# FNet mixing and channel mix on one core: a tile of its own for one mirrored row, and a new order for the opening's products

## The chip, the cores and the metric

The kernel runs on one core of one Trainium2 chip. The metric is the device time of one execution in microseconds (us), as the median of several executions. The engines of the core have these names in the profile: PE is TensorE (matmuls), PEld its weight loads, DVE is VectorE, ACT is ScalarE, POOL is GpSimd, SP is SyncE.

## What is computed

For an input x of 8 batches, 3072 rows and 256 columns the reference takes the real part of a two-dimensional discrete Fourier transform, and puts the result through a channel mix:

```python
X = np.fft.fft(x, axis=1)
X = np.fft.fft(X, axis=2)
x = X.real
x_prev = x shifted by one row, zeros ahead of the first
xk = mu_k * x + (1.0 - mu_k) * x_prev
xr = mu_r * x + (1.0 - mu_r) * x_prev
k = np.maximum(xk @ w_k, 0.0)          # 256 -> 1024
v = k * k @ w_v                        # 1024 -> 256
r = 1.0 / (1.0 + np.exp(-(xr @ w_r)))  # 256 -> 256
out = r * v
```

## The kernel before

**Folding.** The real part of a transform of real data pairs row s with row S - s and column d with column D - d. The kernel therefore loads every batch twice: `load_p` brings the rows as they are (tile `xp`), and `load_m` gathers the mirrored rows (tile `xm`) with an indirect DMA. `fold` adds the two on DVE into the tile `p` (L147 the bulk, L149 the first column again). A batch has two halves, h = 0 with nine rows for each of 96 partitions and h = 1 with eight. The mirrored tile of a half has eight rows of 256 and a ninth behind them, at element `XM0 + 2048`. For h = 0 the ninth comes by a gather of its own, `load_m0`; for h = 1 only a zero written at the start stands there. There are three `xm` tiles in turn, and "slot 0" is the first of them, which the first half of the first batch uses.

The columns of a row are read backwards from the row behind's first element: the bulk add of `fold(0, 0, 1, 4)` reads elements `XM0 + 2048` down to `XM0 + 1025`. Its first element is thus the first of the ninth row. What it adds there is overwritten by the second, small add.

**The transform in stages.** With Cooley-Tukey steps the transform becomes three kinds of products: `a_sum` or `a_item` (L480, L463/460) multiply `p` by the table `w_pm`; `d_half` or `d_item` (L497) multiply the result `a` by the table `w_eo`; `c_item` (L535) multiplies `g_all` by the table `m_cs`. Each stage's result is copied out of PSUM by ACT (L443) or DVE (L441). `halves`, `diff` and `mix_part` on DVE then make the mixed rows for the channel mix.

**Tables.** All tables are made on the chip. Angles are sums of outer products, `outer` (L287), with one row of weights; DVE scales and wraps them (`m_angles`, `m_wrap`, both L249), and ACT takes the sines (`m_sine`, L400). The table `m_cs` comes in three parts of 5, 4 and 5 columns: `(0, NJ1)`, `(NJ1, NJ2)`, `(NJ2, NJ)`. The vectors mu are loaded as rows, reordered by ACT (`mu_rows`, L196), turned into columns by eight tiny fp32 matmuls (`mu_turn`, L203) and copied to `mu_f` by DVE (L205); `mix_part` reads `mu_f`.

**The channel mix.** The steady part has 192 steps over chunks of 512 output rows: `k_piece` (products L615, ACT's relu L625), DVE's `square` (L632), `v_tile` (L653), `r_item` (L639), `v_out` (L663). The next batches' transform is put between by a table of steps (`at`).

**Order.** The order of instructions on each engine is the program's own order: `pin_order` chains them at the end. So an instruction that waits holds back all that stands behind it on its engine. PSUM tiles come in turn from three slots of 1024 columns (`ps_w`, tile `psW`) and two of 512 (`ps_v`, tile `psV`). All input loads are issued by POOL, in one queue. `keep_busy(n)` issues n matmuls of 512 columns on zeros (L180), whose results nobody reads.

The opening of the program, up to the first product of the channel mix, is written out by hand:

```python
    m_sine(0, NJ1)
    m_first()
    mu_rows(1)
    eo_sine()
    eo_rest()
    keep_busy(8)
    fold(0, 0, 1, 4)
    a_sum(0, 0, 0)
    m_outer(NJ1, NJ2)
    fold(0, 0, 5, 4)
    a_sum(0, 0, 4)
    mu_turn()
    loads()
```

Of the kernel before, what the change touches and what calls it, by code (L numbers as in the profile page):

```python
# [10 lines left out]
FP16 = mybir.dt.float16  # L11
# [9 lines left out]
def _v(ap, extra_offset, free_dims):  # L21
    new_ap = [list(ap.ap[0])] + [[s, c] for (s, c) in free_dims]
    return dataclasses.replace(ap, offset=ap.offset + extra_offset, ap=new_ap)
# [16 lines left out]
def kernel(  # L40
# [18 lines left out]
    NJ, NJ1, NJ2 = 14, 5, 9  # L59

    const = ctx.enter_context(tc.tile_pool(name="const", bufs=1))
# [12 lines left out]
    def ps_slot(kind, n, cols):  # L74
        k = ps_n[kind] % n
        ps_n[kind] += 1
        return psum.tile([P, cols], FP32, name=f"ps{kind}{k}", tag=f"ps{kind}{k}", bufs=1)

    def ps_w():
        return ps_slot("W", 3, 1024)  # L80

    def ps_v():
        return ps_slot("V", 2, 512)
# [23 lines left out]
    V = nc.vector  # L107
    XM0 = 257
    xm_sb = [const.tile([96, XM0 + 2306], FP16, name=f"xm{n}") for n in range(3)]
    idx_4 = const.tile([96, 2], UINT32)  # L110
    idx_8 = const.tile([96, B, 2], UINT32)
    idx_0 = const.tile([96, B], UINT32)
# [10 lines left out]
    def gather(dst, src, idx):  # L123
        nc.gpsimd.indirect_dma_start(dst, None, src, bass.IndirectOffsetOnAxis(ap=idx, axis=0))  # L124

    def load_m(b, h, o, n, idx):
        gather(xm_t[b, h][:, XM0 + o:XM0 + o + 256 * n],
               x.rearrange("b (s r) d -> (b s) (r d)", r=n), idx)

    def load_m0(b):  # L130
        load_m(b, 0, 2048, 1, idx_0[:, b:b + 1])

    def load_xh(b, h):
        x_tiles(b, h)
# [5 lines left out]
    def fold(b, h, q0=0, n=0):  # L140

        n = n or 9 - h
        if (b, h) not in p_t:
            p_t[b, h] = p_pool.tile([96, 9, 256], FP16, name="p")
        p, xp, xm = p_t[b, h], xp_t[b, h], xm_t[b, h]
        o = XM0 + 256 * (8 - h - q0)
        V.tensor_tensor(out=p[:, q0:q0 + n], in0=xp[:, q0:q0 + n],  # L147
                        in1=_v(xm, o + 256, [(-256, n), (-1, 256)]), op=ALU.add)
        V.tensor_tensor(out=p[:, q0:q0 + n, 0], in0=xp[:, q0:q0 + n, 0],  # L149
                        in1=_v(xm, o, [(-256, n)]), op=ALU.add)  # L150
# [15 lines left out]
    mu_f = const.tile([P, 2, 2], FP32)  # L166
# [9 lines left out]
    def keep_busy(n, ps=None):  # L176

        ps = ps or ps_v()
        for _ in range(n):
            nc.tensor.matmul(out=ps[:, 0:512], lhsT=zeros, rhs=_v(zeros, 0, [(0, 4), (1, P)]),  # L180
                             start=True, stop=True)

    keep_busy(5)


    mu_row = const.tile([1, 2, 256], FP32)
# [6 lines left out]
    def mu_rows(a):  # L193
        for p0, f0, step, n in (((0, 0, 1, 1), (1, 2, 2, 63), (64, 1, 2, 64)),
                                ((0, 128, 1, 1), (1, 254, -2, 63), (64, 255, -2, 64)))[a]:
            nc.scalar.activation(out=mu_p[:, a, :, p0:p0 + n],  # L196
                                 in_=_v(mu_row, f0, [(256, 2), (step, n)]), func=AF.Copy)

    def mu_turn():
        ps = ps_w()  # L200
        for a in range(2):
            for i in range(2):
                nc.tensor.matmul(out=ps[:, 2 * a + i:2 * a + i + 1], lhsT=mu_p[:, a, i], rhs=unit,  # L203
                                 start=True, stop=True)
        V.tensor_copy(out=mu_f.rearrange("p a i -> p (a i)"), in_=ps[:, 0:4])  # L205

    for h in range(2):
        x_tiles(0, h)
    for xm in xm_sb:
        V.memset(_v(xm, XM0 + 2048, [(256, 2)]), 0.0)  # L210
    iota = nc.gpsimd.iota
    ueo = const.tile([P, 2, 2, 64], INT32)
    w_eo = const.tile([P, 2, 128], FP16)
# [27 lines left out]
    warm = const.tile([P, 1], FP32)  # L241
    nc.scalar.activation(out=warm, in_=zeros[:, 0:1], func=AF.Sin, bias=0.0, scale=1.0)
    mu_rows(0)
    nc.scalar.activation(out=m_cs.rearrange("p c s t -> p (c s t)").bitcast(FP32),
                         in_=_v(zeros.bitcast(FP32), 0, [(0, 2 * NJ), (1, 64)]), func=AF.Copy)

# [15 lines left out]
    def rv(n, o, *dims):  # L262
        return _v(rw, P * n + o, list(dims))
# [21 lines left out]
    def outer(out, rhs):  # L285
        for n, (row, r) in enumerate(rhs):
            nc.tensor.matmul(out=out, lhsT=rw[:, row], rhs=r, start=n == 0, stop=n == len(rhs) - 1)  # L287
# [3 lines left out]
    ps = ps_w()  # L291
# [37 lines left out]
    def m_outer(j0, j1):  # L329
        ps = ang_ps[j0] = ps_w()  # L330
        n = j1 - j0
        for c in range(2):
            outer(ps[:, 512 * c:512 * c + 64 * n],
                  [(Q2, rv(JR, j0, (1, n), (0, 64))), (RR, rv(TR, 0, (0, n), (1, 64))),
                   (PH + c, rv(ONE, 0, (0, n), (1, 64))),
                   (D0 + c, rv(J0, 0, (1, n), (0, 64)))][:4 if j0 == 0 else 3])
# [5 lines left out]
    def m_wrap(j0, j1):  # L342
        ts(ang[:, :, j0:j1], ang[:, :, j0:j1], TURN - 1, ALU.bitwise_and)

    keep_busy(1)
    m_outer(0, NJ1)
    ts(u_w, ps[:, 0:WA + WB], TURN / 96.0, MUL)
    ts(u_w, u_w, TURN - 1, ALU.bitwise_and)
# [49 lines left out]
    def m_sine(j0, j1):  # L398
        for part, odd in ((hi64, 0), (lo64, 1)):
            nc.scalar.activation(  # L400
                out=m_cs.rearrange("p c (j o) t -> p c j o t", o=2)[part, :, j0:j1, odd],
                in_=ang[part, :, j0:j1], func=AF.Sin, bias=m_pi[part], scale=TWO_PI / TURN)

    def m_first():
        nc.scalar.activation(out=_v(m_cs[hi64], 0, [(2 * NJ * 64, 2)]), in_=zeros[hi64, 0:2],
                             func=AF.Copy)
# [17 lines left out]
    def eo_sine():  # L424
        nc.scalar.activation(out=w_eo.rearrange("p a b -> p (a b)"),
                             in_=ueo.rearrange("p a c b -> p (a c b)"), func=AF.Sin,
                             bias=m_pi, scale=TWO_PI / TURN)
# [11 lines left out]
    def evac(out_ap, in_ap, eng):  # L439
        if eng == "V":  # L440
            V.tensor_copy(out=out_ap, in_=in_ap)  # L441
        else:
            nc.scalar.activation(out=out_ap, in_=in_ap, func=AF.Copy)  # L443

    def a_tile(b):
        a_t[b] = y_pool.tile([P, 2, NU, 64], FP16, name="a")
# [21 lines left out]
    def a_sum(b, h, i0, engs="A"):  # L468


        if (h, i0) == (0, 0):
            a_tile(b)
        ps = ps_w()
        for i in range(4):
            parts = [(h, i0 + i + 1 - h, 0, 2 * WA, 0, 1)]
            if h and i0 + i == 7:
                parts = [(0, 0, 0, WA, WA, 1), (1, 7, 1, WA, 1, 2)]
            for half, q, o, n, w, step in parts:
                for k in range(2):
                    nc.tensor.matmul(out=_v(ps, 256 * i + o, [(2 * WA // n, n)]),  # L480
                                     lhsT=p_t[b, half][:, q, 128 * k:128 * k + 128],
                                     rhs=_v(w_pm[0:96], (WA + WB) * k + w,
                                            [(WA + WB, 2), (step, n // 2)]),
                                     start=(k == 0), stop=(k == 1))
            n = 4 // len(engs)
            if i % n == n - 1:
                evac(_v(a_t[b], 8 * h + i0 + i + 1 - n, [(16, 2 * WA), (1, n)]),
                     _v(ps, 256 * (i + 1 - n), [(1, 2 * WA), (256, n)]), engs[i // n])

    def d_units(b, ps, u0, n, bank):  # L490

        for i in range(n):
            for e in range(2):
                o = bank * e + 128 * i
                nc.tensor.matmul(out=ps[:, o:o + 128],  # L497
                                 lhsT=a_t[b][:, e, 2 * (u0 + i):2 * (u0 + i) + 2, :],
                                 rhs=w_eo[:, e], start=True, stop=True)

    def d_evac(ps, u0, n, bank, eng):
        evac(_v(g_all, 256 * u0, [(64, 2), (128, 2 * n), (1, 64)]),
             _v(ps, 0, [(bank, 2), (64, 2 * n), (1, 64)]), eng)
# [8 lines left out]
    def d_half(b, u, ps, eng):  # L512
        d_units(b, ps, u, 2, 256)
        d_evac(ps, u, 2, 256, eng)
# [159 lines left out]

    m_sine(0, NJ1)
    m_first()
    mu_rows(1)
    eo_sine()
    eo_rest()
    keep_busy(8)  # L680
    fold(0, 0, 1, 4)
    a_sum(0, 0, 0)
    m_outer(NJ1, NJ2)
    fold(0, 0, 5, 4)
    a_sum(0, 0, 4)
    mu_turn()
    loads()
    m_angles(NJ1, NJ2)
    m_wrap(NJ1, NJ2)
    keep_busy(4)  # L690
    fold(0, 1, 0, 4)
    a_sum(0, 1, 0)
    fold(0, 0, 0, 1)
    turn_rows()
    fold(0, 1, 4, 4)
    keep_busy(2)
    a_sum(0, 1, 4, "VA")
    m_outer(NJ2, NJ)
    m_angles(NJ2, NJ)
    d_half(0, 0, ps_v(), "A")  # L700
    d_half(0, 2, ps_v(), "V")
    m_wrap(NJ2, NJ)
    c_item(0, 0, 5, "A", True)
    c_item(0, 5, 4, "A", True)
    m_sine(NJ1, NJ2)
    d_item(0, 1)


# [161 lines left out]
```

## Time and profile before

| what | value |
|---|---|
| three executions | 456.34, 457.2, 458.16 us, median 457.2 us |
| the profiled execution | 457.78 us, of it 456.0 us from its first to its last instruction (the span) |
| mean granted clock of TensorE over the span | 0.973 |
| busy PE, DVE, ACT, POOL | 442.3, 360.6, 327.1, 50.9 us |
| PE busy from 100 to 400 us | 300.0 of 300 us |

A slice of the page's second part is a fortieth of the span, 11.4 us. The chain of waits is followed back from the last instruction; a piece of it that names a PE line is time in which PE was the one worked on. Times inside the profile are counted from the first instruction.

### The profile page before, as it was taken

How to read it: one execution, taken by the hardware profiler on the slowest of the kernel's cores; microseconds unless marked ns; L12 is line 12 of the kernel's file. 1: busy time of each engine (PE TensorE's matmuls, PEld its weight loads, DVE VectorE, ACT ScalarE, POOL GpSimd, SP SyncE). 2: the span in 40 equal slices, each digit the busy share in tenths (PEclk: the TensorE clock that was granted, in tenths of full speed). 3: DMA queues.
4: the chain of work that ended last, by engine and by line, in shares of the span. 5: the costliest groups of instructions: out<-in, count | busy, mean ns of one | idle time of the engine just before them, and what ended most of it. 6: DMA issues, size and time to landing. Idle time of an engine off the chain costs nothing.

```text
span 456.0 us, 8500 instructions
## 1 busy us (share of the span) xinstructions
PE 442.3 (97%) x3479; PEld 314.3 (69%) x3479; DVE 360.6 (79%) x529; ACT 327.1 (72%) x369; POOL 50.9 (11%) x65
## 2 busy tenths in 40 slices
PE   8798999999999999999999999999999999999996
PEld 3455677677777777777777777777777777666764
DVE  5357899998789896998879896998879865997453
ACT  6148788777777777777777777777777777666661
POOL 7560213100400012000400010000000000000000
PEclk9657999999999999999999999999999999999999
DMA  7992567623942258222942253322332322333324
GB/s 127 184 175 49 78 141 122 141 55 72 167 111 58 60 100 173 63 64 55 168 117 52 65 95 93 70 64 53 70 69 48 70 63 53 71 70 69 71 64 99
DMA packets 34507, 40.93 MB, mean 90 GB/s; under 512 B 3906, under 2 KB 30788, under 8 KB 34468
## 3 DMA queue, kind: packets, MB, share of 16 engines
q1 hardware_dynamic: 27524, 25.05, 22.7%
q0 software_dynamic: 6784, 15.21, 21.0%
q8 instruction: 27, 0.44, 0.4%
q10 hardware_dynamic: 160, 0.13, 0.1%
q14 instruction: 12, 0.10, 0.1%
HBM read 30.41 MB, written 25.17 MB: 122 GB/s over the span
## 4 chain that ended last, share of the span: by engine, by line
PE 91%; DVE 3%; ACT 2%; DMA 1%; issue 1%; POOL 1%; POOLq 0%; DVEq 0%
PE psV L653 36%; PE psW L615 35%; PE psW L639 9%; PE psW L535 3%; PE psW L497 3%; PE psW L463 2%; PE psW L480 2%; DMA xm<-in_x_dram,idx 1%; ACT rl L625 1%; PE psW L287 1%; DVE k L632 1%; DVE d L559 0%; DVE x L584 0%; POOL xm L124 0%; ACT pq L443 0%
## 5 line engine op out<-in xcount | busy, mean ns | idle before, releaser
L625 ACT ACTIVATE rl<-psW 128x1024 f16<-128x1024 f32 x192 | 196.4, 1024 | 98.8 <-PE psW L615 93.8
L653 PE MATMUL psV<-wv_sb,k 128*128 128x256 f16 x1536 | 199.5, 273 | 0.0
L615 PE MATMUL psW<-x,wk 128*128 128x512 f16 (+1 forms) x776 | 198.1, 379 | 1.2 <-ACT rl L625 0.7
L653 PEld LDWEIGHTS <-k 128*128 128x128 f16 x1536 | 146.5, 98 | 27.9
L632 DVE TENSOR_TENSOR k<-rl 128x2048 f16<-128x2048 f16 (+1 forms) x98 | 117.6, 1201 | 50.9 <-ACT rl L625 50.6
L615 PEld LDWEIGHTS <-wk 128*128 128x128 f16 x776 | 76.3, 98 | 51.9 <-issue 2.4
L663 DVE SCALAR_TENSOR_TENSOR o<-psV,r 128x512 f32<-128x512 f32 (+1 forms) x97 | 66.1, 682 | 16.2 <-PE psV L653 13.7
L584 DVE TENSOR_TENSOR x<-y,t 128x1536 f16<-128x1536 f16 x60 | 57.5, 959 | 2.1
L639 PE MATMUL psW<-wr,x 128*128 128x256 f16 x384 | 49.8, 273 | 0.0
L644 ACT ACTIVATE r<-psW 128x1024 f16<-128x1024 f32 x48 | 48.9, 1018 | 0.8 <-PE psW L639 0.8
L639 PEld LDWEIGHTS <-x 128*128 128x128 f16 x384 | 37.6, 98 | 14.6 <-issue 0.3
L443 ACT ACTIVATE a<-psW 128x832 f16<-128x832 f32 (+1 forms) x32 | 27.2, 849 | 12.5 <-PE psW L480 12.5
L121 POOL DMA_DIRECT2D xp<-in_x_dram x16 | 9.1, 566 | 209.1 <-DVE p L149 184.4
L124 POOL DMA_INDIRECT xm<-in_x_dram,idx x25 | 31.2, 1247 | 7.6 <-issue 6.4
L443 ACT ACTIVATE pq<-psW 128x768 f16<-128x768 f32 (+5 forms) x32 | 27.5, 859 | 1.8 <-PE psW L535 1.7
L443 ACT ACTIVATE g_all<-psW 128x1024 f16<-128x1024 f32 (+3 forms) x39 | 28.0, 722 | 0.0
L147 DVE TENSOR_TENSOR p<-xp,xm 96x2304 f16<-96x2304 f16 (+3 forms) x19 | 20.9, 1102 | 3.9 <-DMA xm<-in_x_dram,idx 3.8
L551 DVE TENSOR_TENSOR y<-pq 128x960 f16<-128x960 f16 (+5 forms) x38 | 18.6, 532 | 5.0 <-ACT pq L443 4.8
L535 PEld LDWEIGHTS <-g_all 128*128 128x128 f16 (+1 forms) x233 | 15.3, 99 | 9.3 <-ACT g_all L443 1.6
L497 PEld LDWEIGHTS <-a 128*128 128x128 f16 x208 | 15.2, 103 | 7.7 <-issue 1.3
L571 DVE TENSOR_SCALAR t<-d,mu_m 128x1536 f16<-128x1536 f16 x32 | 19.6, 614 | 0.0
L535 PE MATMUL psW<-m_cs,g_all 128*128 128x128 f16 (+2 forms) x221 | 18.1, 222 | 1.2 <-ACT g_all L443 1.2
(100 smaller groups left out, 197.5 us busy)
## 6 DMA issues: line engine op xcount, KB each, us to landing
out_dram<-o SPq DMA_DIRECT2D x190, 128.0 KB, 2.4
xp<-in_x_dram POOLq DMA_DIRECT2D x8, 432.0 KB, 6.4
xp<-in_x_dram POOLq DMA_DIRECT2D x8, 384.0 KB, 4.6
wv_sb<-in_moe_w_v_dram POOLq DMA_DIRECT2D x1, 512.0 KB, 9.0
xm<-in_x_dram,idx POOLq DMA_INDIRECT x25, 7.2
out_dram<-o ACTq DMA_DIRECT2D x2, 64.0 KB, 2.0
out_dram<-o SPq DMA_DIRECT2D x2, 64.0 KB, 2.2
wk<-in_moe_w_k_dram,row_i POOLq DMA_INDIRECT x4, 7.0
```

The lines of the kernel that those rows point to most:

```text
L124: nc.gpsimd.indirect_dma_start(dst, None, src, bass.IndirectOffsetOnAxis(ap=idx, axis=0))
L443: nc.scalar.activation(out=out_ap, in_=in_ap, func=AF.Copy)
L497: nc.tensor.matmul(out=ps[:, o:o + 128], lhsT=a_t[b][:, e, 2 * (u0 + i):2 * (u0 + i) + 2, :], rhs=w_eo[:, e], start=True, stop=True)
L535: nc.tensor.matmul(out=ps[0:m, o:o + 64 * k], lhsT=g_all[:, u, 128 * min(f, 1):128 * min(f, 1) + m], rhs=m_cs[:, f % 2, sl:sl + k], start= ...
L584: V.tensor_tensor(out=dst, in0=_v(y_t[b], 64 * (NSL * a + lo + 3 * m), [(1, n)]), in1=_v(x_t["t", a], 64 * lo, [(1, n)]), op=ALU.subtract ...
L615: nc.tensor.matmul(out=st["k", ds][:, 512 * hs + lo:512 * hs + hi], lhsT=wk_sb[m][a][:, 128 * fc:128 * fc + 128], rhs=xk[:, a, 512 * i + l ...
L625: nc.scalar.activation(out=st["rl"][:, 2 * ds:2 * ds + 2], in_=st["k", ds].rearrange("p (f t) -> p f t", f=2), func=AF.Relu, bias=0.0, sca ...
L632: V.tensor_tensor(out=k2_t[c][:, lo:hi], in0=r, in1=r, op=ALU.mult)
L639: nc.tensor.matmul(out=ps[:, 256 * tb:256 * tb + 256], lhsT=x_t[b, 1, m][:, a, 512 * i + 128 * tb: 512 * i + 128 * tb + 128], rhs=wr_sb[m] ...
L644: nc.scalar.activation(out=st["r", c], in_=ps, func=AF.Sigmoid)
L653: nc.tensor.matmul(out=st["v", tb - h][:, 256 * h:256 * h + 256], lhsT=k2_t[c][:, fc, 128 * tb:128 * tb + 128], rhs=wv_sb[:, fc], start=(f ...
L663: V.scalar_tensor_tensor(out=o.rearrange("p a b -> p (a b)")[:, 0:256 * n], in0=st["v", t0][:, 0:256 * n], scalar=16.0, in1=st["r", c][:, ...
```

## The change

It touches the opening alone, in these parts:

1. The ninth mirrored row of the first half of the first batch is gathered into a tile of its own, `xm_00`, instead of the first `xm` tile. `fold(0, 0, 0, 1)` reads it there. The other folds and the other batches are as before.
2. `keep_busy` at the very start has 8 matmuls instead of 5; the one ahead of `m_outer(0, NJ1)` goes; the block of 8 ahead of the first `a_sum` becomes 7; the blocks of 4 and 2 between the later `a_sum` go.
3. `m_outer(NJ1, NJ2)` goes from between the first two `a_sum` to a place ahead of the block of 7.
4. `mu_rows(1)` goes forward on ACT to stand beside `mu_rows(0)`. `mu_turn` goes behind `m_wrap(NJ1, NJ2)` and `m_sine(NJ1, NJ2)` in the program, and its copy on DVE to `mu_f` is taken out of it and put behind the last `a_sum`.
5. `m_sine(NJ1, NJ2)` goes from behind the first two `c_item` to a place right behind its `m_wrap`.
6. `d_half(0, 0)` and `d_half(0, 2)` now stand ahead of `m_outer(NJ2, NJ)` and `m_angles(NJ2, NJ)`.

```diff
+    xm_00 = const.tile([96, 514], FP16)
...
     def load_m0(b):
-        load_m(b, 0, 2048, 1, idx_0[:, b:b + 1])
+        if b == 0:
+            gather(xm_00[:, 1:257], x.rearrange("b s d -> (b s) d"), idx_0[:, 0:1])
+        else:
+            load_m(b, 0, 2048, 1, idx_0[:, b:b + 1])
...
         o = XM0 + 256 * (8 - h - q0)
+        if (b, h, q0) == (0, 0, 0):
+            xm, o = xm_00, 1
...
-    keep_busy(5)
+    keep_busy(8)
...
-        V.tensor_copy(out=mu_f.rearrange("p a i -> p (a i)"), in_=ps[:, 0:4])
+        return ps
...
+    V.memset(xm_00[:, 257:258], 0.0)
...
     mu_rows(0)
+    mu_rows(1)
...
-    keep_busy(1)
     m_outer(0, NJ1)
...
     m_first()
-    mu_rows(1)
     eo_sine()
     eo_rest()
-    keep_busy(8)
+    m_outer(NJ1, NJ2)
+    keep_busy(7)
     fold(0, 0, 1, 4)
     a_sum(0, 0, 0)
-    m_outer(NJ1, NJ2)
     fold(0, 0, 5, 4)
     a_sum(0, 0, 4)
-    mu_turn()
     loads()
     m_angles(NJ1, NJ2)
     m_wrap(NJ1, NJ2)
-    keep_busy(4)
+    m_sine(NJ1, NJ2)
+    mu_ps = mu_turn()
     fold(0, 1, 0, 4)
     a_sum(0, 1, 0)
     fold(0, 0, 0, 1)
     turn_rows()
     fold(0, 1, 4, 4)
-    keep_busy(2)
     a_sum(0, 1, 4, "VA")
+    V.tensor_copy(out=mu_f.rearrange("p a i -> p (a i)"), in_=mu_ps[:, 0:4])
+    d_half(0, 0, ps_v(), "A")
+    d_half(0, 2, ps_v(), "V")
     m_outer(NJ2, NJ)
     m_angles(NJ2, NJ)
-    d_half(0, 0, ps_v(), "A")
-    d_half(0, 2, ps_v(), "V")
     m_wrap(NJ2, NJ)
     c_item(0, 0, 5, "A", True)
     c_item(0, 5, 4, "A", True)
-    m_sine(NJ1, NJ2)
     d_item(0, 1)
```

## The prediction

> **What bounds the kernel now.** First the page's second part, for where PE lacks work or clock:
>
> ```profile
> PE   8798999999999999999999999999999999999996
> ...
> PEclk9657999999999999999999999999999999999999
> ```
>
> From the fifth slice (46 us) on PE is full at full clock. Time is to be had in the opening alone, and an opening shorter by x ends the kernel earlier by x, if nothing later is short of data. Next, the chain of waits there (start, length, what):
>
> ```profile
> 6.12 6.79 DMA xm<-in_x_dram,idx
> ...
> 13.04 0.70 DVE p L147
> ...
> 14.00 0.89 PE psW L480 x8
> 14.89 1.38 PE psW L287 x6
> 16.26 1.50 PE psW L480 x8
> 17.76 1.81 PE psW L203 x8
> ...
> 19.59 0.16 DVE mu_f L205
> ...
> 20.88 0.70 DVE p L147
> ...
> 23.40 0.85 PE psV L180 x2
> ```
>
> The first fold waits for the gather issued at 6.12, the ninth row's; the eight rows that its sums need were issued at 2.53 and landed 7.1 later, at 9.6. Then PE works in its order, with the angles (L287) and mu (L203) between the sums, and DVE's copy of mu stands ahead of the next fold, whose data had landed by 12.5 (issue 4.48, 8.0 to landing). The waits of the opening say the same:
>
> ```profile
> DVE mu_f L205 <- PE psW L203: 4.9, 1, 4.9
> ...
> DVE p L147 <- DMA xm<-in_x_dram,idx: 3.8, 1, 3.8
> ```
>
> Last the clock. Its record changes at 11.46 (up), 14.87 (down), 35.35, 42.18 and 45.59, all whole multiples of 3.41 us apart. The busy times by these stretches (length, then PE, PEld, DVE, ACT, POOL, clock, DMA share, GB/s):
>
> ```profile
> 4.63:8.05 3.42, 3.21 (x14) 1.74 (x15) 1.94 (x10) 1.20 (x3) 2.78 (x5) 1.00 0.91 160
> 8.05:11.46 3.41, 3.09 (x8) 0.80 (x6) 1.12 (x3) 2.83 (x7) 2.74 (x9) 1.00 1.03 189
> 11.46:14.87 3.41, 0.87 (x9) 0.70 (x10) 1.63 (x4) 0.28 (x3) 2.93 (x4) 1.00 1.08 187
> ...
> 21.70:25.11 3.41, 3.12 (x14) 2.05 (x15) 2.00 (x12) 0.86 (x1) 2.05 (x3) 0.50 1.04 168
> ```
>
> The column of 1.00 ahead of 11.46 is no clock: the 512-column matmuls start every 0.43 there (7.94 to 10.08 is five of them), as at 0.50. 4.63 to 8.05 was busy, but with one-row weights, and brought no full clock; 8.05 to 11.46, with 2.90 of 128-row work (85%), did. 21.70 to 25.11 did not: 2.08 with 96 of 128 rows and 0.85 with 128, by rows 71%. So a stretch counts by rows; it raises the clock somewhere from 71 to 85%. A stretch with 32% (38.77 to 42.18, five k products of 0.216 by their rate there) lost it, one with PE busy for 2.46 (45.59 to 49.00) kept it.
>
> **Parts with one answer.** `mu_rows(1)` (0.6 of ACT) goes to 3.0, where ACT is free from 4.6 to 5.85: nothing. Blocks of zeros whose removal saves only PE time that was waiting (the one of L180 at 3.87): nothing. The longer first block runs from 1.0 to 4.4 (8 x 0.43); the outer products behind it, at 3.24 before, end about 5.1, and DVE reads them at 5.24 at the earliest, since it writes rows until 5.3: nothing, and at most 0.2 if this is short. The new memset: 0.06 of DVE in the free start. POOL issues the same number of loads in the same order; the second batch's second half, which waited for a fold until 22.45, can go at 18.4, but DMA was saturated then (share over 1 in every us from 15 to 36), and one queue serves all: nothing for slot 0, whose last gather lands at 13.8 (7.33 and 6.5).
>
> **The first fold.** It starts at 9.75 (9.6 and the 0.13 that it took at 12.91) instead of 13.04; DVE is free from 9.2. First sums at 10.7 instead of 14.0: 3.3 off the path, if PE is free. Its block of seven stands behind the six angle products (1.28). With the clock's boundaries as in this trace, 1.0 to 4.4 fills 94% of 1.22 to 4.63, so the clock is full to 8.05, the block done at 9.7. At other boundaries all of it runs at half rate: 7.7 + 1.28 + 7 x 0.43 = 12.0, and the first sums lose 1.3 of the 3.3.
>
> DVE now adds while POOL issues loads (9.65 to 12.8). The add of 13.86 ran beside POOL's gather of 13.74 to 14.70 in 0.68, that of 20.88 beside an idle POOL in 0.69: no price. The Trainium skill (SBUF — State Buffer, the section with the port table) says that a DVE instruction with two SBUF inputs and a GpSimd instruction reading SBUF block each other for a whole instruction. The two adds do not show it. By the rule up to 0.95 could come back at each of three folds, 2.9 in all, and the sum would be 452.1.
>
> **From first sum to the first `c_item`,** 14.00 to 29.76 before, at half clock (starts of neighbours subtracted): the angle products between go (1.38); four zeros and the wait behind them, 19.49 to 21.83, go (2.34), since DVE, without mu's copy, folds at 10.57 and 12.65, and that half is ready at 13.55, PE at 15.3 after mu's matmuls (1.8); the two zeros go (0.85), since the last fold is ready at 15.55 and PE comes at 16.7. Against this, the first sums ran in 0.82 at full clock and now take 1.39 (-0.57), and behind the last copy of `a` PE does `d_half` (1.03) and the angles (1.60) in 3.06 instead of 2.93 (-0.13): ACT's copy (0.6), which hid behind the angles, now stands open, and the angles hide the copy of `g_all` instead. 1.38 + 2.34 + 0.85 - 0.57 - 0.13 = 3.9. `c_item` starts at 29.76 - 3.3 - 3.9 = 22.5.
>
> `m_sine(NJ1, NJ2)` (1.45) now runs at 14.6 on ACT, between copies that end at 14.6 and start at 16.9: hidden. From `c_item` on PE was full up to 38.57, so the 1.45 that ACT gains at 32.33 is worth nothing.
>
> **The clock's share.** At this trace's boundaries no stretch from 8.05 to 25.11 holds over 65% (8.05 to 11.46: zeros 1.65, sums 0.57): half clock, 7.2 in all. At boundaries in the middle of the block of seven, zeros and the sums behind them fill over 85% and the clock rises between 12 and 14: after the loss of 1.3 each set of eight sums saves 0.69, mu's about 0.9, the later pieces up to 2, bounded by the folds at 13.55 and 15.55: 8 to 10. Where it rises nowhere: 7.2 - 1.3 = 5.9. One profile doesn't tell where boundaries fall in other runs. I take 8.0, nearest the first two cases, and keep 5.9 and 10.
>
> **Sum.** The profiled execution took 457.8, 0.6 above the median: 449.8 for it, 449.2 against the median.
>
> **Rivals.** *Full clock throughout.* PE is busy from 1.0 to 9.7 and never waits 2 us; were rows no matter, the clock stayed up. Then only data and copies bind: last fold 15.55, sums and copies to 18.1, `c_item` at 19.35, 10.4 earlier, and about 2 more from its products, zeros and k products at full rate until DVE binds: 12.4, or 444.8. Against it: 4.63 to 8.05 and 21.70 to 25.11 above. The Trainium skill (TensorE: Matmul & The Clock Gate, "Why this matters for your kernels") asks only for 4 us of continuous work. The trace disagrees where that work has one row or 96.
>
> *The fold stays tied.* The eight-row gather shares the queue and perhaps the count that the fold waits for; then the first sums stay at 14.0, and only the 3.9 is left: 453.3. For it: what the fold really waits for is inferred. Against: each landing has its own time in the trace.
>
> *Taken back by data.* The next batch's fold came at 44.97, its data at 25.0; the second half's at 53.48, data at 31.7; the next weights land by 34.6. Slack 18 and more: 457 only if something unseen binds.
>
> *Slower.* With the six zeros between the sums gone, the stretches around the first k products could miss the share that raises the clock, and the steady part start at half clock. A step has 0.86 of k and 0.87 of v products at full rate, so each costs 1.73 more; to end 0.5% slower the 8.0 and 2.3 more must go, six steps, 21 us of PE work at half clock: 449.2 + 6 x 1.73 = 459.6. Against it: every stretch with over 85% raised the clock, four zeros and k products still stand together, and steps at half clock are full.
>
> **Numbers.** Forecast 0.78, full clock 0.08, tied 0.07, taken back 0.02, slower 0.05. The range reaches from just above full clock, 445.0, to the tied case, 453.5; it leaves out part of the full clock and the last two, some 0.12. About 0.5%, 2.3 us, is what a measurement of this kernel can tell from no change: faster 0.93, same 0.02, slower 0.05.
>
> **What would show it.** In the changed profile: first L147 near 9.75, released by the gather of 2.53; first L480 at 10.7 to 12.0; no L205 wait of DVE ahead of the second half's fold, which starts by 13; first L535 at 19.5 to 24; L400 near 15; L625 first at 31 to 33 instead of 39. Wrong if the first L480 is still at 14, if the clock stays at 0.50 beyond the first k products, or if DVE or ACT show a new wait of over 1 us between 10 and 22 on mu or the sines.

## The result: about 1.5% faster, a little less than forecast

| | before | after | ratio (95% interval) |
|---|---|---|---|
| first comparison | 457.51 us | 451.47 us | 0.9869 (0.9834 to 0.9905) |
| repeated | 456.97 us | 449.41 us | 0.9835 (0.9805 to 0.9864) |
| repeated again | 457.37 us | 449.47 us | 0.9817 (0.9783 to 0.9850) |

One of the eleven runs of the kernel before in the second comparison took 738.54 us at a mean granted clock of 0.653, and its ratio leaves that run out. The sixteen runs of the changed kernel lie between 446.71 and 452.51, their median is 449.9. The first profiled execution took 450.17, its span 448.4: 7.6 less than before. The forecast of 449.2 lies 2.3 below the first median and within 0.3 of the two later ones.

The page's second part after the change, PE and its clock:

```profile
PE   9889999999999999999999999999999999999995
...
PEclk9778999999999999999999999999999999999999
```

PE is fuller in the first four slices, and from the fifth to the last but one it is as full as before. The first relu of the steady part starts at 31.29 instead of 38.96, 7.7 earlier, and the span is 7.6 shorter: what the opening gains goes through to the end. ACT before and after:

```profile
38.96 2.81 ACT L625 ACTIVATE rl<-psW 128x1024 f16<-128x1024 f32 x3
...
31.29 2.81 ACT L632 ACTIVATE rl<-psW 128x1024 f16<-128x1024 f32 x3
```

The chain of waits in the opening (start, length, what):

```profile
4.50 8.52 DMA xm<-in_x_dram,idx
...
13.53 0.70 DVE p L153
...
16.55 0.70 PE psW L487 x4
...
19.15 0.55 ACT a L450
...
20.78 1.71 PE psW L295 x6
22.49 1.84 PE psW L542 x15
```

The first fold is no longer on it. The chain now begins with the gather for the second half (issued at 4.50) and goes over DVE's folds; mu's products and the copy of mu are gone from it. The line numbers have moved: L487 are the sums (L480 before), L153 the folds, L542 the `c_item` (L535). The first `c_item` starts at 22.42 by the timeline (the chain counts it from 22.49), where before it was this line:

```profile
29.76 1.91 PE L535 MATMUL psW<-m_cs,g_all 128*128 128x64 f16 x15 [0.26 <-ACT g_all L443]
```

The first fold and the first sums in the timeline of DVE and of PE:

```profile
10.27 0.69 DVE L153 TENSOR_TENSOR p<-xp,xm 96x1024 f16<-96x1024 f16 x1 [0.83 <-DMA xm<-in_x_dram,idx]
```

```profile
9.05 3.17 PE L186 MATMUL psV<-zeros 128*128 128x512 f16 x7
12.01 2.40 PE L487 MATMUL psW<-w_pm,p 96*128 96x208 f16 x16
14.34 1.05 PE L209 MATMUL psW<-unit,mu_p 1*128 1x1 f32 x8
```

The fold starts 2.8 earlier than before, but PE comes only when the seven zeros end, at 12.0. The clock record rises at 13.67, falls at 17.09, rises at 27.33, falls once more at 34.15 and is up from 37.57 to 447.16. The two stretches around the rise (length, busy PE, PEld, DVE, ACT, POOL, clock, DMA share, GB/s):

```profile
10.25:13.67 3.42, 3.42 (x15) 2.06 (x14) 2.78 (x7) 1.22 (x6) 3.11 (x4) 1.00 1.11 188
13.67:17.09 3.42, 3.07 (x28) 2.49 (x27) 2.57 (x12) 3.38 (x5) 2.81 (x3) 1.00 0.96 130
```

The first holds zeros and sums (1.79 of zeros and 1.63 of sums with 96 of 128 rows, by rows 88%), the second sums and mu's products at full clock (1.6 of sums, by rows about 35%), and it loses the clock again. The 1.00 of the first stretch is still the missing record; its rate is half.

### The profile page after: what moved, and what is told of

Same layout as the page of the kernel before. It is cut to its first block, busy times and chain, and to the rows that moved or that the text cites. A ratio compares the mean times of both kernels' runs of the same rounds, so it can differ in the third digit from the quotient of the medians.

```text
span 448.4 us, 8492 instructions
## 1 busy us (share of the span) xinstructions
PE 437.5 (98%) x3474; PEld 312.4 (70%) x3474; DVE 361.0 (81%) x530; ACT 327.1 (73%) x369; POOL 51.6 (12%) x65
## 4 chain that ended last, share of the span: by engine, by line
PE 91%; DVE 3%; ACT 2%; DMA 2%; issue 1%; POOL 0%; POOLq 0%; DVEq 0%
PE psV L660 36%; PE psW L622 36%; PE psW L646 9%; PE psW L542 3%; PE psW L504 3%; DMA xm<-in_x_dram,idx 2%; PE psW L470 2%; ACT rl L632 1%; PE psW L487 1%; DVE k L639 1%; DVE d L566 0%; DVE x L591 0%; ACT pq L450 0%; PE psW L295 0%; PE psW L186 0%
## 5 line engine op out<-in xcount | busy, mean ns | idle before, releaser
L153 DVE TENSOR_TENSOR p<-xp,xm 96x2304 f16<-96x2304 f16 (+3 forms) x19 | 20.9, 1102 | 1.3 <-DMA xm<-in_x_dram,idx 1.3
L542 PEld LDWEIGHTS <-g_all 128*128 128x128 f16 (+1 forms) x233 | 15.3, 99 | 9.4 <-ACT g_all L450 1.1
L542 PE MATMUL psW<-m_cs,g_all 128*128 128x128 f16 (+2 forms) x221 | 18.1, 222 | 0.9 <-ACT g_all L450 0.9
```

What stands on the lines that cost most here:

```text
L542: nc.tensor.matmul(out=ps[0:m, o:o + 64 * k], lhsT=g_all[:, u, 128 * min(f, 1):128 * min(f, 1) + m], rhs=m_cs[:, f % 2, sl:sl + k], start= ...
```

## Experiments

**The tile alone.** The kernel before, with `xm_00`:

```diff
+    xm_00 = const.tile([96, 514], FP16)
...
+        if b == 0:
+            gather(xm_00[:, 1:257], x.rearrange("b s d -> (b s) d"), idx_0[:, 0:1])
...
+        if (b, h, q0) == (0, 0, 0):
+            xm, o = xm_00, 1
...
+    V.memset(xm_00[:, 257:258], 0.0)
```

> The kernel before with the own tile for the ninth row alone. Theory (two separate gains, tile and order): the first fold starts at 10.2 instead of 13.04, released by the eight-row gather; the first sums start at 11.1 (the block of eight ends there) instead of 14.0; everything behind, mu's copy ahead of the second half's fold included, comes 2.8 us earlier: 454.7 against 457.5. Rival A (the order does it all, since the wait for mu's copy binds anyway): under 0.5 us of gain. Rival B (the tile does it all): 6 us, 451.5. Rival C (the fold stays tied): first fold at 13, no gain.

Measured: 451.53 against 457.26, ratio 0.9866 (0.9833 to 0.9900), single runs from 450.55 to 452.68. The PE timeline, of the slowest of the four:

```profile
7.57 3.60 PE L186 MATMUL psV<-zeros 128*128 128x512 f16 x8
10.96 1.55 PE L487 MATMUL psW<-w_pm,p 96*128 96x208 f16 x8
12.44 0.82 PE L294 MATMUL psW<-rw 1*128 1x256 f16 x6
13.20 0.89 PE L487 MATMUL psW<-w_pm,p 96*128 96x208 f16 x8
14.01 1.05 PE L209 MATMUL psW<-unit,mu_p 1*128 1x1 f32 x8
```

The times of the theory came (fold 9.59, sums 10.96, 3.0 earlier). Its 454.7 is 3.2 too high, since a second gain came that it did not have. With the wait gone the sums follow the zeros at once, the clock rises at 12.34, and the angles, the second sums and mu's products take 0.76, 0.81 and 0.98 where they took 1.38, 1.49 and 1.80; the first sums, at half, lose 0.66. First `c_item` at 25.12, 4.6 earlier: 3.0 and 1.6. The size is that of rival B, and in the first comparison the whole change (451.47) was no faster than this. The reason is not rival B's: DVE still waits 3.81 for mu's products here, and the order alone gains as well, as the next run shows.

**The order alone.** The changed kernel, the ninth row in the shared tile:

```diff
-    xm_00 = const.tile([96, 514], FP16)
...
-        if (b, h, q0) == (0, 0, 0):
-            xm, o = xm_00, 1
...
```

> The changed kernel without the own tile: the ninth row goes to the shared tile again. Theory: first fold at 13, first sums at 14.0, and only the order's share is left, 3.2 to 3.9 us: 453.6 to 454.3 against 457.5; the second half's fold starts at about 16 instead of 20.9. Rival A (the order does it all): 451.5. Rival B (the tile does it all): 457 to 458.

Measured: 452.79, ratio 0.9897 (0.9868 to 0.9925), first `c_item` at 26.14, 3.6 earlier, span 3.9 shorter. PE:

```profile
14.01 2.96 PE L480 MATMUL psW<-w_pm,p 96*128 96x208 f16 x16 [3.63 <-DVE p L149]
16.89 1.86 PE L203 MATMUL psW<-unit,mu_p 1*128 1x1 f32 x8
```

The second half's fold starts at 15.71 instead of 20.88. The theory's places hold, all at half clock, and the profiled execution (453.83) lies in its range; the median is 0.8 below it. Each part alone gives 4.5 to 5.7 us and both together 6.0 to 7.9, less than the sum. In the profiles the parts bring the first `c_item` 4.6 and 3.6 forward, and both together 7.3, and 6.4 and 8.1 in the two repeats further down. In two of these three the block of seven ends at 12.0, where the block of eight ended at 11.0, which is 1.0 of what is missing. The medians lack more than that; why was not traced.

**Four zeros instead of seven.**

```diff
-    keep_busy(7)
+    keep_busy(4)
```

> The changed kernel with four 512-column zeros instead of seven ahead of the first sums. Theory (the seven hold the first sums up: they end at 12.0 where the fold is ready at 11.2): first sums at 11.2, 0.8 us earlier; the clock then rises in no stretch ahead of 17, so the sums run at half rate and up to 1.9 us come back: between 0.8 faster and 1.1 slower than the changed kernel's 451.5. Rival D (the zeros set nothing, data does): no difference, first sums at 12. Rival E (the zeros are what keeps the opening fast): 2 us or more slower, 453.5 and above.

Measured: 449.61, ratio 0.9832 (0.9806 to 0.9858), its four runs within 0.4. First sums at 10.89 instead of 12.01, but the last sums start at 16.21 instead of 16.55: they wait for the last fold, so only 0.5 of the 1.1 reaches the first `c_item` (21.97). The clock rose all the same (13.16): the expectation that it would not was wrong. Beside all sixteen runs of the changed kernel the time is not told apart.

**The clock by rows.** Zeros with a chosen number of rows ahead of everything (one execution, 502.08 us):

```diff
...
+    for rows, n in ((1, 24), (96, 24), (P, 24), (96, 48), (1, 48)):
+        zeros_rows(rows, n, probe_ps)
     keep_busy(5)
```

> The kernel before with matmuls of 512 columns on zeros put ahead: 24 with one row, 24 with 96 rows, 24 with 128, 48 with 96, 48 with one row (blocks of about 10 us, without a gap). Nothing else differs; it is some 50 us longer. Theory (the clock counts rows): no rise in the first block; the rise comes in the block of 128 rows, or, if the share that raises it lies under 75%, in the first block of 96; it is kept through the second block of 96 and lost within two stretches of 3.41 us in the last block of one row. Rival (busy time counts, whatever the rows): the rise comes within 7 us of the first matmul, and the clock is kept to the end.

By 0.43 and 0.216 a matmul the blocks begin at 1.0, 11.2, 19.6, 24.8 and 35.1. The record rises at 17.66, falls at 38.14. The stretches:

```profile
7.42:10.83 3.41, 3.41 (x10) 1.12 (x8) 0.00 (x0) 0.00 (x0) 2.72 (x9) 1.00 1.05 196
10.83:14.25 3.42, 3.42 (x9) 1.03 (x8) 0.00 (x0) 0.00 (x0) 3.12 (x4) 1.00 1.13 189
14.25:17.66 3.41, 3.41 (x9) 1.21 (x8) 0.00 (x0) 0.00 (x0) 2.49 (x4) 1.00 1.16 149
...
34.72:38.14 3.42, 3.42 (x17) 1.36 (x16) 0.00 (x0) 0.00 (x0) 0.00 (x0) 1.00 0.00 0
38.14:41.55 3.41, 3.41 (x10) 1.17 (x9) 0.00 (x0) 0.00 (x0) 0.00 (x0) 0.50 0.00 0
```

PE is busy throughout. One row brings no rise in 10 us, 96 rows bring it with the first stretch that they fill, and one row loses it with the first stretch that it fills nearly alone. Rows count, and a filled stretch of 96 rows, 75%, is enough. With the 71% of the kernel before, which were not, the share that raises the clock lies between 71 and 75%.

**The copy of mu back ahead of the second half's fold.**

```diff
     mu_ps = mu_turn()
+    V.tensor_copy(out=mu_f.rearrange("p a i -> p (a i)"), in_=mu_ps[:, 0:4])
     fold(0, 1, 0, 4)
...
-    V.tensor_copy(out=mu_f.rearrange("p a i -> p (a i)"), in_=mu_ps[:, 0:4])
```

> The changed kernel with DVE's copy of mu right behind mu's products again, ahead of the second half's fold. Theory (the copy held DVE): that fold starts behind mu's products, at 15.5 instead of 13.5, the last fold at 17.6 instead of 15.7, and the end comes about 2 us later: 453.5. Rival (PE's order holds the sums anyway): the sums of the second half start behind mu's products in both, under 0.5 us.

Measured: 451.13, 1.7 above the changed kernel of the same comparison (449.41). DVE's wait is back, in the list of waits from 8 to 20 us:

```profile
DVE mu_f L697 <- PE psW L209: 2.8, 1, 2.8
```

The fold starts at 15.28 instead of 13.53, the last one at 17.30 instead of 15.70, the first `c_item` at 24.32 instead of 22.42: 1.9. These places are as the theory has them. The span is only 1.0 longer than that of the first profile (449.4 against 448.4), because this execution does not lose the clock a second time behind the first k products (it is up from 30.26 on).

**The zeros back between the sums,** run in two comparisons:

```diff
     mu_ps = mu_turn()
+    keep_busy(4)
...
     fold(0, 1, 4, 4)
+    keep_busy(2)
     a_sum(0, 1, 4, "VA")
```

> The changed kernel with the blocks of four and two zeros back between the later sums. Theory (they now stand on the path): 0.9 to 1.7 us for the four, up to 0.9 for the two, 453 to 454. Rival (they raise the clock and pay for themselves): 451.5 or less, with a record of full clock from 17 on.

> The changed kernel with the blocks of four and two zeros back, again. Theory (zeros cost 2 us where the clock is at half, and where it is up they keep it up and give 4 to 5): single runs fall into two groups, near 446 and from 449 to 452.5; the median beats the changed kernel by 1 us or more. Rival (the two runs at 445.9 were chance): median within 1 us of the changed kernel's.

Measured: 447.46 and 447.43, 2.0 below the median of the changed kernel both times (ratios 0.9791, 0.9752 to 0.9830, and 0.9796, 0.9753 to 0.9839). The intervals overlap those of the changed kernel. The ten runs go from 445.39 to 452.60, and their mean, 448.5, is only 0.65 below the 449.1 of the twelve runs beside them: that the zeros gain is not clear of the spread. In the first profile, of the slowest run of its four (452.45), the clock is at half from 7.72 to 31.61, and there the zeros cost what was expected; PE:

```profile
15.62 1.89 PE L186 MATMUL psV<-zeros 128*128 128x512 f16 x4
...
25.64 1.91 PE L542 MATMUL psW<-m_cs,g_all 128*128 128x64 f16 x15
```

In the second the record is up from 10.46 to 20.70 and `c_item` starts at 20.29. The number of the first expectation was wrong for the median; its rival has the number, but not the record, in this profile. The two groups of the second are not clean, and one run of its six lies near 446: of the ten runs three lie from 445.4 to 445.9, three from 447.3 to 447.5, four from 449 to 452.6.

**Three more zeros, ahead of `d_half`,** with the blocks of four and two as above:

```diff
     V.tensor_copy(out=mu_f.rearrange("p a i -> p (a i)"), in_=mu_ps[:, 0:4])
+    keep_busy(3)
     d_half(0, 0, ps_v(), "A")
```

> As the last, with three more zeros between the second half's last sums and the first products with w_eo, where PE waits 0.63 for ACT's copy. Theory: at full clock they hide in that wait (3 x 0.216) and hold the clock through the stretch behind, so that more runs are near 446; at half clock they cost 3 x 0.43 - 0.63 = 0.7. Median at or below the last kernel's. Rival (the clock is settled earlier): median 0.3 to 0.7 above the last kernel's.

Measured: 446.09, ratio 0.9783 (0.9749 to 0.9816), four of six runs from 445.68 to 446.09. It is the fastest of all, and these four runs lie below all sixteen of the changed kernel. In the profile (445.68) the record rises at 12.32 and stays up to 442.40, 1.5 ahead of the end. PE:

```profile
13.68 1.05 PE L209 MATMUL psW<-unit,mu_p 1*128 1x1 f32 x8
...
18.39 0.85 PE L186 MATMUL psV<-zeros 128*128 128x512 f16 x3
...
20.69 1.22 PE L542 MATMUL psW<-m_cs,g_all 128*128 128x64 f16 x15
```

The first sums start at 12.01, as in the changed kernel; nine zeros more, and `c_item` starts 1.7 earlier and takes 1.22 instead of 1.91. The first relu comes 3.0 earlier (28.25) and the end 4.5. The last 1.5 come from behind the first relu. There PE waits for ACT in every profile. In the changed kernel this wait falls into one stretch of 3.41 us, which loses the clock; here the boundary of two stretches cuts it, and neither loses the clock. The changed kernel, then this run:

```profile
30.74:34.15 3.41, 1.25 (x7) 0.66 (x7) 3.23 (x7) 3.36 (x4) 0.20 (x1) 1.00 1.15 211
...
25.97:29.39 3.42, 1.98 (x15) 1.25 (x14) 2.63 (x5) 3.38 (x6) 2.81 (x4) 1.00 1.06 205
29.39:32.80 3.41, 2.69 (x23) 1.67 (x23) 2.99 (x7) 3.21 (x4) 1.32 (x2) 1.00 1.15 197
```

The profiles of mu's copy put back and of the first run with the zeros back do not lose it there either. In these three the first to the sixth relu take 6.2, in all others 7.8 to 7.9. How often a boundary falls so is not known.

**The last fold first on DVE,** with four zeros ahead of the first sums:

```diff
-    fold(0, 0, 0, 1)
-    turn_rows()
     fold(0, 1, 4, 4)
+    fold(0, 0, 0, 1)
...
     V.tensor_copy(out=mu_f.rearrange("p a i -> p (a i)"), in_=mu_ps[:, 0:4])
+    turn_rows()
```

> The changed kernel with four zeros instead of seven ahead of the first sums, and on DVE the second half's last fold ahead of the single row's fold, with the rows for the turn table behind the copy of mu. Theory (after the change DVE's order sets when the last sums start, 16.2 with four zeros): last fold done at 15.0 instead of 16.2, PE's last sums and all behind 1 us earlier, 448.6 against 449.6 for the block of four alone. Rival (the landing of the last gather, about 14, or PE binds there): 449.6, no difference.

Measured: 449.56 beside 449.41 of the changed kernel. The last fold starts at 14.17, right behind the landing of its gather:

```profile
14.17 0.69 DVE L153 TENSOR_TENSOR p<-xp,xm 96x1024 f16<-96x1024 f16 x1 [0.16 <-DMA xm<-in_x_dram,idx]
```

In the profile `c_item` starts at 20.92, 1.05 ahead of the block of four alone, and the span is 0.7 shorter: the place is right. The median shows no gain, three runs at 450.3 to 451.0 having a mean clock of 0.972, against 0.983 to 0.986 of the other three.

**The first block of five again.**

```diff
-    keep_busy(8)
+    keep_busy(5)
...
+    keep_busy(1)
     m_outer(0, NJ1)
```

> The changed kernel with the first blocks of zeros as before the change: five at the very start, one ahead of the first angles. Theory (an early rise of the clock is lost over the one-row products, and then leaves the block of seven at the wrong place: in the second record of the changed kernel it ended 1.2 us ahead of the first sums and brought no rise): no early rise, the rise comes at 12 to 14 in more runs, median 0.5 to 1 us below the changed kernel's. Rival (the first block of eight is worth what it costs): the same within 0.5, or slower.

Measured: 449.07 beside 449.47, single runs from 446.52 to 451.27: not decided. In its one profile the clock rises at 13.71, and no rise stands ahead of that.

**The changed kernel again,** twice:

> The changed kernel again, for its spread and a second clock record. Theory (its time depends on where the clock's stretches of 3.41 us fall in the opening, which differs from run to run): single runs spread from 450 to 452.5 as before, and the first L542 lies at 22.4 again only if the clock rises at a similar place; with no rise between 10 and 17 it lies at 23.5 to 24. Rival (the spread comes from elsewhere, the steady part): the opening is the same to 0.2 us, and the span differs.

> The changed kernel a third time, beside the three below on the same chip. Theory (its time hangs on where the clock's stretches fall): single runs from 447 to 452.5, median near 450.2, the median of the ten runs so far.

The second record has an early rise (4.24 to 7.65) and then half clock to 28.13; PE:

```profile
11.21 2.96 PE L487 MATMUL psW<-w_pm,p 96*128 96x208 f16 x16 [1.18 <-DVE p L155]
...
23.34 1.91 PE L542 MATMUL psW<-m_cs,g_all 128*128 128x64 f16 x15
```

Single runs lie from 446.97 to 450.95, below the 450 to 452.5 of the expectation; its place for `c_item` without a rise, 23.5 to 24, holds to 0.2. The third record rises at 13.57 and has its `c_item` at 21.70; the median, 449.47, is 0.7 below the expected one. First relu at 32.15 and 30.87, spans 449.2 and 447.9: in all three profiles the span is shorter by what the first relu is earlier (7.7, 6.8, 8.1 against 7.6, 6.8, 8.1). What differs between these three executions is the opening. The fastest ones (446.7 to 447.3) were not profiled.

## Why the prediction was right, point by point

- **First fold: right.** It is released by the eight-row gather, and starts at 10.27, 10.24 and 9.68 in the three profiles, where I had 9.75; the landing moves from run to run (9.59 for the fold with the tile alone, 9.94 with the block of four). The rival of the fold that stays tied is out.
- **First sums at 10.7 to 12.0: right.** 12.0 in two profiles, 11.2 in that with the early rise. The loss of up to 1.3 behind the block of seven came. The block of four shows that taking it away brings only 0.5, because the last fold binds next. That the first profile's `c_item` lies at 22.42, where the sum has 22.5, is luck: the sum has first sums at 10.7 and half clock behind them; the sums came 1.3 later, and a rise of the clock gave as much back.
- **From the first sums to `c_item`: right at half clock.** The second profile has it: 11.21 to 23.34, 12.1, against 15.8 before; 3.6 where the sum had 3.9. The copy of mu was the item that held DVE (1.9 by its return), and `m_sine` ran at 15.34, between copies, unnoticed.
- **The clock's share: mechanism right, size too high.** Rise at 13.57 and 13.67 gave 8.1 and 7.6, no rise there 6.8; I had 8 to 10, 7.2, and 8.0 for the whole. The three mean 7.5. The term was sized for a clock that stays up behind 14; in both profiles it fell 3.4 later, with the stretch of sums and mu's one-row products at about 35%. From the last sums to `c_item` (17.91 to 22.42) these profiles take 4.5, as does the second at half clock: the later pieces, priced at up to 2, saved nothing. The folds bound more than in the sum, too: the second half's starts at 13.53, 13.49 and 12.93, where I had 12.65, in the first profile behind a landing at 13.0 instead of 12.5. So the 8.0 was chosen between cases of which both came out lower, and it is partly luck that 449.2 lies within 0.3 of two medians.
- **The removed zeros: right at half clock, incomplete beside it.** The sum took them, with a wait, as 2.34 and 0.85 saved. At half clock the zeros cost 2.6: from the first sums to `c_item` 14.7 with them, 12.1 without, at nearly the same record. The sum has no term for what they do to the clock at full rate: I asked only which waits they covered. With them three of ten runs come below every run of the changed kernel, and three lie at 451.5 or above. The median is 2.0 lower, but the spread does not let this gain be called shown; with nine zeros it is clearer (four of six runs below all sixteen).
- **Full clock throughout, 444.8 as a rival.** The changed kernel did not get there, as forecast. With nine zeros more, four runs come near it: 445.7 to 446.1. So the rival's price was nearly right, although the profiled one of them is at half rate up to 12.32 and has its `c_item` at 20.69 where the rival has 19.35; its condition was rows in every stretch, not continuous work. The Trainium skill's advice (TensorE: Matmul & The Clock Gate, "Why this matters for your kernels") of 4 us without a gap failed on the 10 us of one-row matmuls.
- **No price for adds beside loads: right for the adds.** The folds take 0.67 to 0.69 after the change as before. What gets longer is the gather, as the last section has it; the list of waits shows none that came of it.
- **Taken back by data, slower:** neither showed. The spans follow the first relu, and the clock rose at 27.22 to 28.13 in all three profiles, with the first k products. It is lost once more for 3.41 us at 34.05 to 34.96, as before at 42.18. One reading beside this was wrong, and nothing hangs on it: the DMA share in the kernel before is not over 1 in every us from 15 to 36 (0.83 from 24 to 25, 0.64 from 27 to 28).

Where the first comparison's four runs drew their clock is not known, since only one was profiled; that they lie 2 us above the later ones is put down to that without proof.

## What to carry to other kernels

A tile shared by two transfers ties a reader to both, even if it touches one element of the second and overwrites it later; a small tile apart frees it. Ahead of a copy that only something much later needs, look at what is queued behind it. Filler matmuls are to be judged by the rows in each stretch of the clock and not only by the wait that they fill: taken out at half clock they save their length, and they may cost more where the clock would have been up.

## What the runs showed of the hardware that was not expected

- One-row matmuls count as nearly idle: no rise in 10 us of them, and the clock lost in the first stretch of 3.41 us with them.
- The share by rows that raises the clock lies between 71% (not raised, kernel before) and 75% (raised, 96 rows). The one that keeps it lies near 38%: about 35% lost it (13.67 to 17.09 above), and so did about 38% (13.57 to 16.98 in the third profile of the changed kernel), while about 39% kept it (10.46 to 13.87 in the second profile with the zeros back, 1.04 of sums by rows and 0.31 of zeros). Both are worked out from counts of matmuls and their rates, so the gap is no wider than their error. The same count for every stretch in the first 60 us of the fourteen profiles agrees: the 38 that raised the clock hold 75% or more, the 72 that left it at half 72% or less; the 25 that lost it hold 38% or less, the 109 that kept it 39% or more.
- PE's busy time does not tell this share, and columns count as well as rows. This stretch of the kernel before has PE busy for 92%, all with 128 rows, and did not raise the clock:

```profile
28.53:31.94 3.41, 3.15 (x28) 2.06 (x28) 2.25 (x5) 1.53 (x3) 2.80 (x4) 0.50 1.05 190
```

  By its matmuls' columns (512 take 0.43 at half rate) it holds 76%. Five of the matmuls, in the first `c_item`, have weights of a single column; with the columns of the weights counted too, as in the count above, 62% are left. So the prediction's argument that every stretch with over 85% raised the clock does not hold for busy time.
- An indirect load that POOL issues while DVE adds two tensors takes longer, and the add does not. After the change the gathers of 11.17 and 15.76, issued with half a us of a fold still to run, take 1.41 and 1.33, the others of the opening 0.90 to 1.03. In all fourteen profiles 166 gathers start with 0.3 us or more of such an add still to run; their median is 1.44, that of the 227 with no two-input instruction of DVE running at their start 0.94.
- Where the stretches begin differs from run to run, and with it the opening of one kernel: first relu from 30.87 to 32.15 in the three profiles of the changed one. Its single runs go from 446.7 to 452.5; the ends of that range were not profiled.
